# Linear attention with a rational FFN on one core: k'v of two head pairs in one visit to TensorE

## The chip, the cores and the metric

The kernel runs on one core of a Trainium2 chip. The metric is the device time of one execution in microseconds (us). Before the change the median of three runs is 900.26 us (900.21 to 900.27). The engines are named as in the profile: PE is TensorE (PEld its weight loads), ACT is ScalarE, DVE is VectorE, POOL is GpSimd, and SP is the engine whose queue issues nearly all transfers here.

## The reference

Eight batches of eight heads, 576 positions, head size 64. Attention without a softmax, an RMS norm over the head, and a feed-forward layer whose activation is a rational function:

```python
kv = np.einsum('bhsd,bhse->bhde', k, v)
out = np.einsum('bhsd,bhde->bhse', q, kv)
rms = np.sqrt(np.mean(out * out, axis=-1, keepdims=True) + 1e-06)
attn = out / rms * g_norm
x = attn.transpose(0, 2, 1, 3).reshape(4608, 512)
h = x @ w_in                                   # 512 -> 2048
P = a[0] + a[1] * h + a[2] * h**2 + a[3] * h**3
Q = 1.0 + np.abs(b[0]) * np.abs(h) + np.abs(b[1]) * h**2
return (P / (Q + 1e-06)) @ w_out               # 2048 -> 512
```

All inputs and the output are float32.

## The kernel before

**Tiles and slots.** The 4608 tokens are nine tiles of 512 (`NTILE`, numbered `t` = 0 to 8). The 2048 columns of the hidden layer are 16 chunks of 128 (`NF`), and one chunk of one tile is a *slot*; there are 144 of them, run in order. In a slot PE makes `gemm1` of the next slot (the 128x512 tile `h`, four pieces of the contraction) and `gemm2` of the slot two back (`LAG = 2`; four sub-tiles `acc`). ACT and DVE meanwhile turn `h` into the rational function `g` (`ew_a` to `ew_d`). From tile 1 on every operand of the two products is split into a high part in fp32r and a remainder (`xh`, `xl`; `gh`, `gl`; and so for the weights), and a product is three matmuls: 12 for `gemm1` and 12 for `gemm2` in a slot. Tile 0 uses plain float32 matmuls; a plain float32 matmul shows as two records in the profile.

**Attention.** While tile `t` goes through its 16 slots, the attention of tile `t + 1` is made in between, by the table `attention` (`attention0` in tile 0), which puts steps into slots. The eight heads are four pairs `p` (`NPAIR`), and the tile is made of parts of two batches, `t - 1` and `t` (64·t tokens of the older one). The steps:

- `att_kv`, in slots 0, 2, 4, 6 for pairs 0 to 3 (1, 3, 5, 7 in tile 0): the product k'v of batch `t`, pair `p`. For each of five pieces `c` of 128 positions and each head `j` of the pair, one plain float32 matmul of 128 rows by 64 columns, so ten matmuls (20 records), into columns 0 to 63 of the PSUM tile `kvp`; head `j` goes to partitions 64·j to 64·j + 63. Then ACT makes the high part `qh` of the query tile and two casts `kvh` (`split_kv`), and DVE the remainders `kvl` and `ql`. Only batches 1 to 7 are left by then (`NB` = 8; batch 0 is done in a prologue), so tile 8 has queries and no k'v.
- `att_o`, one slot later: the product q·k'v of that pair (`op`), its square and its copy `xf`. It shares one PSUM buffer (tag `at`) with `kvp`.
- `att_ms`, `att_rstd`, `att_rd`, `att_rb`, `att_norm` in slots 8 to 13: the norm, whose factor goes through DRAM to be broadcast. In slot 14, `split` makes the high and low part of the finished `x`.

Work that a step leaves to DVE is a closure that `ew_c` calls between its own three instructions (`rest[0]` to `rest[2]`; `fillat` gives the place). Nothing reorders the instructions: each engine runs them in the order written.

**Loads.** One 640 KB transfer brings k and v of a pair into `kvm` (one buffer, `bufs=1`), one of 256 KB the queries into `qr` (one buffer). `fetch_next` issues both for the next pair on SP's queue: right after the pair's `qh` is made, or in tile 0, where no split of q is made, after its `att_o`. SP waits at an issue until the buffer is free, and later issues wait behind it.

Names in a row, such as `kvp_0_1936`, end in the pair (or sub-tile, or chunk) and a serial number; the tile number isn't shown.

Of the kernel before, what the change touches and what calls it, by code (L numbers as in the profile page):

```python
# [7 lines left out]
F32 = mybir.dt.float32  # L8
F32R = mybir.dt.float32r
# [5 lines left out]
ALU = mybir.AluOpType  # L15
# [9 lines left out]
def linear_attention_then_rational_ffn(  # L25
# [9 lines left out]
    nc = tc.nc  # L35
    PE, ACT, DVE, POOL = nc.tensor, nc.scalar, nc.vector, nc.gpsimd

    NB, NPAIR = kv.shape[:2]
    NT, DM = out.shape
    NF = w_in.shape[0]  # L40
    P = 128
    D = 64
    S = NT // NB
    TW = 512
    NTILE = NT // TW
# [7 lines left out]
    work = ctx.enter_context(tc.tile_pool(name="work", bufs=2))  # L53
# [3 lines left out]
    ps_at = ctx.enter_context(tc.tile_pool(name="ps_at", bufs=2, space=PSUM))  # L57
# [14 lines left out]
    kvf = wpool.tile([P, 2, NPAIR, P], F32, tag=f"f{NF - 1}", name="kvf")  # L72
# [40 lines left out]
    kvh = [const.tile([P, P], F32R, name=f"kvh{i}") for i in range(NKV)]  # L113
    kvl = [const.tile([P, P], F32R, name=f"kvl{i}") for i in range(NKV)]
# [4 lines left out]
    def f32(t):  # L119
        return t.bitcast(F32)  # L120
# [26 lines left out]
    def at_slot(step, k):  # L147
        return [u for u in units if schedule[u][step] == k]
# [19 lines left out]
    def fetch_w(u):  # L168
        kind, c = u
        k = units.index(u) % NG  # L170
        raws[u] = wpool.tile([P, 2 * DM], I64, tag=f"g{k}", name=f"raw_{kind}{c}")
        src = w_in[c:c + 2].rearrange("c p k f -> p c (k f)") if kind == "wi" else \
            w_out[c:c + 2].rearrange("c p f -> p c f")
        to = raws[u].rearrange("p (c f) -> p c f", c=2)
        for js in ((slice(0, 1), slice(1, 2)) if u in units[:2] else (slice(0, 2),)):
            nc.sync.dma_start(to[:, js], src[:, js])
# [84 lines left out]
    def split_kv(t, p, ps):  # L261
        n = kvslot[t, p] = (t * NPAIR + p) % NKV
        for j in range(2):
            js = slice(j * D, (j + 1) * D)
            ACT.copy(kvh[n][js, js], ps[js, 0:D])
            if t == 1:
                ACT.copy(kvf[js, 1, p, js], ps[js, 0:D])

        if t == 1:

            for j in range(2):
                js = slice(j * D, (j + 1) * D)
                POOL.tensor_tensor(kvl[n][js, js], kvf[js, 1, p, js], f32(kvh[n][js, js]), ALU.subtract)
            return None

        def rest():
            for j in range(2):
                js = slice(j * D, (j + 1) * D)
                DVE.tensor_tensor(kvl[n][js, js], ps[js, 0:D], f32(kvh[n][js, js]), ALU.subtract)
        return rest  # L280

    def newton_rstd(ms, r, r2):
# [20 lines left out]
        return rest  # L303

    xs, x = {}, {}
    kvq, qs, sqs, rs, rbs, xf = {}, {}, {}, {}, {}, {}

    def fetch_kvq(t, p):
        if t < NB:
            m = work.tile([P, 2, 5, P], F32, tag="kvm", name=f"kvm_{t}_{p}", bufs=1)  # L310
            nc.sync.dma_start(m, kv[t, p])
        else:
            m = None
        q = work.tile([P, TW], F32, tag="qr", name=f"qr_{t}_{p}", bufs=1)
        nc.sync.dma_start(q, qT[p, :, t * TW:(t + 1) * TW])
        kvq[t, p] = m, q

    def fetch_next(t, p):
        if p + 1 < NPAIR:
            fetch_kvq(t, p + 1)  # L320
        elif t + 1 < NTILE:
            fetch_kvq(t + 1, 0)

    def att_kv(t, p):
        m, q = kvq.pop((t, p))
        if t < NB:
            ps = ps_at.tile([P, TW], F32, tag="at", name=f"kvp_{t}_{p}", bufs=1)
            for c in range(5):
                for j in range(2):
                    js = slice(j * D, (j + 1) * D)  # L330
                    PE.matmul(ps[js, 0:D], m[:, 0, c, js], m[:, 1, c, js], start=(c == 0), stop=(c == 4))  # L331
        if t == 1:
            qs[t, p] = q
        else:
            qh = work.tile([P, TW], F32R, tag="qh", name=f"qh_{t}_{p}", bufs=1)
            ql = work.tile([P, TW], F32R, tag="ql", name=f"ql_{t}_{p}", bufs=1)
            ACT.copy(qh, q)
            qs[t, p] = qh, ql
            fetch_next(t, p)
        split_v = split_kv(t, p, ps) if t < NB else None  # L340

        def rest():
            if split_v:
                split_v()
            if t > 1:
                DVE.tensor_tensor(ql, q, f32(qh), ALU.subtract)
        return rest

    def att_o(t, p):
        ps = ps_at.tile([P, TW], F32, tag="at", name=f"op_{t}_{p}", bufs=1)  # L350
        q = qs.pop((t, p))
        n0 = D * t
        for bt, cs in ((t - 1, slice(0, n0)), (t, slice(n0, TW))):
            if cs.start == cs.stop:
                continue
            if t == 1:
                PE.matmul(ps[:, cs], kvf[:, bt, p], q[:, cs], start=True, stop=True)  # L357
                continue
            qh, ql = q
            n = kvslot[bt, p]  # L360
            PE.matmul(ps[:, cs], kvh[n], ql[:, cs], start=True, stop=False)  # L361
            PE.matmul(ps[:, cs], kvl[n], qh[:, cs], start=False, stop=False)  # L362
            PE.matmul(ps[:, cs], kvh[n], qh[:, cs], start=False, stop=True)  # L363
        sq = work.tile([P, TW], F32, tag="at", name=f"sq_{t}_{p}", bufs=4)
        xf[t, p] = xpool.tile([P, TW], F32, tag=f"xf{p}", name=f"xf_{t}_{p}")
        ACT.activation(sq, ps, AF.Square)
        ACT.copy(xf[t, p], ps)
        sqs[t, p] = sq
        if t == 1:
            fetch_next(t, p)  # L370

    def att_ms(t, _):
        rs[t] = ps_at.tile([P, TW], F32, tag="ms", name=f"ms_{t}", bufs=1)
# [39 lines left out]

    attention = {s: [] for s in range(NF)}
    for p in range(NPAIR):
        attention[2 * p].append((att_kv, p))
        attention[2 * p + 1].append((att_o, p))
        attention[(11, 12, 13, 13)[p]].append((att_norm, p))
    attention[8].append((att_ms, 0))
    attention[9].append((att_rstd, 0))  # L420
    fillat = {att_norm: 1, att_kv: 1, att_o: 1, att_rstd: 2}
    attention[10] += [(att_rd, 0), (att_rb, 0), (att_rb, 1)]

    fillat0 = {att_kv: 1}
    attention0 = {s: [] for s in range(NF)}
    for f, at in ((att_kv, [1, 3, 5, 7]), (att_o, [2, 4, 6, 8]), (att_ms, [9]), (att_rstd, [9]), (att_rd, [10]), (att_rb, [11, 11]), (att_norm, [12, 12, 13, 13])):
        for p, k in enumerate(at):
            attention0[k].append((f, p))

# [166 lines left out]
    first_x(NPAIR - 2)  # L596
    for u in at_slot(0, -1)[:1]:
        fetch_w(u)
    fetch_kvq(1, 0)
    for u in at_slot(0, -1)[1:]:  # L600
        fetch_w(u)
    ms0 = ps_at.tile([P, TW], F32, tag="ms", name="ms_0", bufs=1)
# [22 lines left out]
    for p in range(NPAIR):  # L625
        pool, tag, bufs = ((ps_h, "h", 2), (ps_h, "h", 2), (ps_at, "at", 1), (ps_at, "ms", 1))[p]
        rb = pool.tile([P, TW], F32, tag=tag, name=f"rb_0_{p}", bufs=bufs)
        ps = slice(p * Q4, (p + 1) * Q4)
# [11 lines left out]
    for i, (t, c) in enumerate(slots[:-1]):  # L640
# [6 lines left out]
        rest = {0: [], 1: [], 2: []}  # L647
# [83 lines left out]
```

## Time and profile before

| | |
|---|---|
| median of three runs | 900.26 us (900.21 to 900.27) |
| the profiled execution: its own time, its span | 900.13 us, 898.4 us |
| PE busy | 890.4 us, 99% of the span |
| DVE, ACT, POOL busy | 772.9 us (86%), 692.5 us (77%), 113.9 us (13%) |
| granted clock of PE | 0.999 |
| moved by DMA | 74.30 MB, 83 GB/s on average |

The profile is that of one execution. The span is the time from its first to its last record; 1.73 us of the execution's own time lie outside it. Rows of the timeline give the start and the duration of an instruction in us, the engine, the line of the kernel, the operation, the tile written and those read, and how many like it stand in the row. Matmuls are pipelined, so what a matmul costs is the distance from its start to the next one's, not its duration. In such rows `kvp<-kvm` are the k'v products, `h<-x,parts` and `acc<-woh,gl` the two big products, `op<-ql,kvh` q·k'v.

### The profile page before, as it was taken

How to read it: one execution, taken by the hardware profiler on the slowest of the kernel's cores; microseconds unless marked ns; L12 is line 12 of the kernel's file. 1: busy time of each engine (PE TensorE's matmuls, PEld its weight loads, DVE VectorE, ACT ScalarE, POOL GpSimd, SP SyncE). 2: the span in 40 equal slices, each digit the busy share in tenths (PEclk: the TensorE clock that was granted, in tenths of full speed). 3: DMA queues.
4: the chain of work that ended last, by engine and by line, in shares of the span. 5: the costliest groups of instructions: out<-in, count | busy, mean ns of one | idle time of the engine just before them, and what ended most of it. 6: DMA issues, size and time to landing. Idle time of an engine off the chain costs nothing.

```text
span 898.4 us, 11765 instructions
## 1 busy us (share of the span) xinstructions
PE 890.4 (99%) x4294; PEld 680.1 (76%) x4294; DVE 772.9 (86%) x1223; ACT 692.5 (77%) x1171; POOL 113.9 (13%) x95
## 2 busy tenths in 40 slices
PE   8999999999999999999999999999999999999998
PEld 5444446878887888878887888788878887888886
DVE  3987898889978898889878997799788988898887
ACT  5898878887876788677867787768767887777665
POOL 2644465653000000000000000000000000000000
PEclk9999999999999999999999999999999999999999
DMA  9964046764131203220320122111302020201001
GB/s 367 351 254 147 25 94 165 170 132 99 41 130 41 49 25 105 83 49 1 130 75 19 37 94 78 42 49 42 129 13 49 0 71 13 49 1 47 1 1 47
DMA packets 26266, 74.30 MB, mean 83 GB/s; under 512 B 2592, under 2 KB 2592, under 8 KB 26208
## 3 DMA queue, kind: packets, MB, share of 16 engines
q1 hardware_dynamic: 23328, 64.10, 21.3%
q0 software_dynamic: 2304, 8.39, 5.1%
q10 hardware_dynamic: 576, 1.05, 0.3%
q8 instruction: 34, 0.56, 0.2%
q14 instruction: 24, 0.20, 0.1%
HBM read 55.58 MB, written 9.57 MB: 73 GB/s over the span
## 4 chain that ended last, share of the span: by engine, by line
PE 95%; DVE 2%; DMA 1%; ACT 1%; issue 0%; SPq 0%; ACTq 0%; DVEq 0%
PE h L448 14%; PE h L450 13%; PE h L449 13%; PE acc L511 13%; PE acc L513 13%; PE acc L512 13%; PE acc L507 6%; PE h L444 5%; PE kvp L331 2%; DMA first<-in_first_dram 1%; PE ms L375 1%; PE op L362 1%; PE op L363 1%; PE op L361 1%; PE op L357 0%
## 5 line engine op out<-in xcount | busy, mean ns | idle before, releaser
L458 ACT ACTIVATE d<-h 128x512 f32<-128x512 f32 x143 | 85.6, 599 | 157.0 <-PE h L450 155.2
L448 PE MATMUL h<-x,parts 128*128 128x512 f32 (+1 forms) x516 | 205.0, 397 | 0.0
L450 PE MATMUL h<-x,parts 128*128 128x512 f32 (+1 forms) x516 | 200.5, 389 | 0.0
L512 PE MATMUL acc<-wol,gh 128*128 128x512 f32 x508 | 197.7, 389 | 0.0
L460 DVE SCALAR_TENSOR_TENSOR q<-d,b1abs,q 128x512 f32<-128x512 f32 x143 | 107.1, 749 | 95.5 <-ACT q L459 95.4
L449 PE MATMUL h<-x,wil 128*128 128x512 f32 (+1 forms) x388 | 150.5, 388 | 0.0
L511 PE MATMUL acc<-parts,gl 128*128 128x512 f32 x384 | 149.4, 389 | 0.0
L513 PE MATMUL acc<-parts,gh 128*128 128x512 f32 x384 | 149.4, 389 | 0.0
L448 PEld LDWEIGHTS h<-x,parts 128*128 128x128 f32 x516 | 96.9, 188 | 25.9 <-DVE gl L495 5.9
L471 ACT ACTIVATE d<-q,bias 128x512 f32<-128x512 f32 x143 | 105.3, 737 | 12.7 <-DVE q L460 10.9
L450 PEld LDWEIGHTS h<-x,parts 128*128 128x128 f32 x516 | 96.9, 188 | 20.6
L461 ACT ACTIVATE u<-h,na 128x512 f32<-128x512 f32 x143 | 112.0, 783 | 0.0
L512 PEld LDWEIGHTS acc<-wol,gh 128*128 128x128 f32 x508 | 95.4, 188 | 19.8
L472 ACT ACTIVATE d<-d,bias 128x512 f32<-128x512 f32 x143 | 103.6, 725 | 4.7
L468 DVE SCALAR_TENSOR_TENSOR u<-u,na,h 128x512 f32<-128x512 f32 x143 | 106.1, 742 | 0.6
L478 DVE SCALAR_TENSOR_TENSOR u<-u,na,d 128x512 f32<-128x512 f32 x143 | 106.5, 744 | 0.0
L462 DVE TENSOR_TENSOR u<-u,h 128x512 f32<-128x512 f32 x143 | 97.8, 684 | 0.8
L476 DVE SCALAR_TENSOR_TENSOR q<-q,d 128x512 f32<-128x512 f32 x143 | 98.3, 687 | 0.2 <-ACT d L472 0.2
L459 ACT ACTIVATE q<-h,abg 128x512 f32<-128x512 f32 x143 | 97.9, 685 | 0.0
L484 DVE SCALAR_TENSOR_TENSOR u<-q,u 128x512 f32<-128x512 f32 x127 | 91.7, 722 | 2.4
L495 DVE TENSOR_TENSOR gl<-u,gh 128x512 fp32r<-128x512 f32 x127 | 86.8, 683 | 0.0
L449 PEld LDWEIGHTS h<-x,wil 128*128 128x128 f32 x388 | 73.0, 188 | 13.8
(146 smaller groups left out, 1234.6 us busy)
## 6 DMA issues: line engine op xcount, KB each, us to landing
kvm<-in_kv_dram SPq DMA_DIRECT2D x28, 640.0 KB
raw_wo<-in_w_out_dram SPq DMA_DIRECT2D x8, 1024.0 KB
qr<-in_qT_dram SPq DMA_DIRECT2D x32, 256.0 KB
out_dram<-ob SPq DMA_DIRECT2D x16, 512.0 KB
rb<-rd SPq DMA_DIRECT2D x28, 256.0 KB
raw_wi<-in_w_in_dram SPq DMA_DIRECT2D x6, 1024.0 KB
wol<-wow POOLq DMA_DIRECT2D x8, 512.0 KB, 5.2
wil<-wiw POOLq DMA_DIRECT2D x6, 512.0 KB, 4.6
```

The source lines that it names most:

```text
L448: PE.matmul(ph, wh, xl, start=(kc == 0), stop=False)
L449: PE.matmul(ph, wl, xh, start=False, stop=False)
L450: PE.matmul(ph, wh, xh, start=False, stop=(kc == NPAIR - 1))
L460: q_made = DVE.scalar_tensor_tensor(q, d, b1abs, q, ALU.mult, ALU.add)
L461: ACT.activation(u, ph, AF.Identity, bias=na[:, 2:3], scale=na[:, 3:4])
L468: DVE.scalar_tensor_tensor(u, u, na[:, 1:2], ph, ALU.add, ALU.mult)
L471: ACT.activation(d, q, AF.Ln, bias=bias[:, 2:3], scale=QSC)
L472: ACT.activation(d, d, AF.Exp, bias=bias[:, 3:4], scale=-1.0)
L478: DVE.scalar_tensor_tensor(u, u, na[:, 0:1], d, ALU.add, ALU.mult)
L511: PE.matmul(o, gl[:, ss], wh, start=(c == 0), stop=False)
L512: PE.matmul(o, gh[:, ss], wl, start=False, stop=False)
L513: PE.matmul(o, gh[:, ss], wh, start=False, stop=(c == NF - 1))
```

## The change

The two k'v products of pairs 0 and 1 are made in one visit in slot 0 of a tile, and those of pairs 2 and 3 in slot 4 (`att_kv2`), each into its own 64 columns of one PSUM tile. The queries keep their slots 0, 2, 4 and 6 (`att_q`). k and v get two buffers, by the parity of the pair (`kvm0`, `kvm1`), and are fetched two pairs at a time; the queries are fetched for themselves. In tile 0, where the attention of tile 1 is made, k'v stays one pair to a visit (`att_kv1`).

```diff
 def split_kv(t, p, ps):        # ps is now the 64 columns of the pair
-            ACT.copy(kvh[n][js, js], ps[js, 0:D])
+            ACT.copy(kvh[n][js, js], ps[js])
...
+    def fetch_kv(t, p):
+        kvms[t, p] = work.tile([P, 2, 5, P], F32, tag=f"kvm{p % 2}", name=f"kvm_{t}_{p}", bufs=1)
+        nc.sync.dma_start(kvms[t, p], kv[t, p])
+
+    def fetch_q(t, p):
+        qrs[t, p] = work.tile([P, TW], F32, tag="qr", name=f"qr_{t}_{p}", bufs=1)
+        nc.sync.dma_start(qrs[t, p], qT[p, :, t * TW:(t + 1) * TW])
+
+    def fetch_first_kv(t):
         if t < NB:
+            for p in range(2):
+                fetch_kv(t, p)
...
+    def kv_products(t, ps, k, p):
+        m = kvms.pop((t, p))
+        for c in range(5):
+            for j in range(2):
+                js = slice(j * D, (j + 1) * D)
+                PE.matmul(ps[js, k * D:(k + 1) * D], m[:, 0, c, js], m[:, 1, c, js], start=(c == 0), stop=(c == 4))
...
+    def att_kv2(t, g):
+        if t >= NB:
+            return None
+        ps = ps_at.tile([P, TW], F32, tag="at", name=f"kvp_{t}_{g}", bufs=1)
+        for k in range(2):
+            kv_products(t, ps, k, 2 * g + k)
+        if g == 0:
+            for p in (2, 3):
+                fetch_kv(t, p)
         else:
+            fetch_first_kv(t + 1)
+        splits = [split_kv(t, 2 * g + k, ps[:, k * D:(k + 1) * D]) for k in range(2)]
         def rest():
+            for f in splits:
+                f()
+        return rest
+
+    def att_q(t, p):
+        q = qrs.pop((t, p))
+        qh = work.tile([P, TW], F32R, tag="qh", name=f"qh_{t}_{p}", bufs=1)
+        ql = work.tile([P, TW], F32R, tag="ql", name=f"ql_{t}_{p}", bufs=1)
+        ACT.copy(qh, q)
+        qs[t, p] = qh, ql
+        fetch_next_q(t, p)
...
 in att_o:
         if t == 1:
-            fetch_next(t, p)
+            if p + 1 < NPAIR:
+                fetch_kv(t, p + 1)
+            else:
+                fetch_first_kv(t + 1)
+            fetch_next_q(t, p)
...
     for p in range(NPAIR):
-        attention[2 * p].append((att_kv, p))
+        if p % 2 == 0:
+            attention[2 * p].append((att_kv2, p // 2))
+        attention[2 * p].append((att_q, p))
         attention[2 * p + 1].append((att_o, p))
```

PE's order around slot 0 of the tile in which batch 3 is prepared, before and then after (`kvp` is the PSUM tile of k'v, `kvm` the loaded k and v, `acc` and `h` the results of `gemm2` and `gemm1`):

```order
L511 MATMUL acc_3_1141<-woh_1648,gl_14_1875 128x512
L512 MATMUL acc_3_1141<-wol_1677,gh_14_1874 128x512
L513 MATMUL acc_3_1141<-woh_1648,gh_14_1874 128x512
L331 MATMUL kvp_0_1936<-kvm_0_1427 64x64 x10
L448 MATMUL h_1_1956<-x_0_1853,parts_847 128x512
L449 MATMUL h_1_1956<-x_0_1853,parts_859 128x512
```

```order
L538 MATMUL acc_3_1159<-woh_1648,gl_14_1875 128x512
L539 MATMUL acc_3_1159<-wol_1677,gh_14_1874 128x512
L540 MATMUL acc_3_1159<-woh_1648,gh_14_1874 128x512
L332 MATMUL kvp_0_1936<-kvm_0_1306 64x64 x10
L332 MATMUL kvp_0_1936<-kvm_1_1308 64x64 x10
L475 MATMUL h_1_1970<-x_0_1853,parts_849 128x512
L476 MATMUL h_1_1970<-x_0_1853,parts_861 128x512
```

The ten matmuls of pair 1, from the second buffer, now follow those of pair 0 directly. On the same engine, two slots later, before and after:

```order
L512 MATMUL acc_3_2055<-wol_929,gh_0_1983 128x512
L513 MATMUL acc_3_2055<-parts_913,gh_0_1983 128x512
L331 MATMUL kvp_1_2068<-kvm_1_1950 64x64 x10
L448 MATMUL h_3_2088<-x_0_1853,parts_847 128x512
L449 MATMUL h_3_2088<-x_0_1853,parts_859 128x512
```

```order
L539 MATMUL acc_3_2071<-wol_931,gh_0_1999 128x512
L540 MATMUL acc_3_2071<-parts_915,gh_0_1999 128x512
L475 MATMUL h_3_2089<-x_0_1853,parts_849 128x512
L476 MATMUL h_3_2089<-x_0_1853,parts_861 128x512
L477 MATMUL h_3_2089<-x_0_1853,parts_849 128x512
```

Here `gemm1` now follows `gemm2` with nothing in between. On DVE, at the end of that slot 0 (`kvl` and `ql` are the remainders of k'v and q, `u` the rational function's numerator), before and after:

```order
L478 SCALAR_TENSOR_TENSOR u_0_1911<-u_0_1911,na,d_0_1909 128x512
L279 TENSOR_TENSOR kvl_131<-kvp_0_1936,kvh_125 64x64 x2
L346 TENSOR_TENSOR ql_0_1948<-qr_0_1429,qh_0_1947 128x512
L484 SCALAR_TENSOR_TENSOR u_0_1911<-q_0_1910,u_0_1911 128x512
L460 SCALAR_TENSOR_TENSOR q_1_1976<-d_1_1975,b1abs,q_1_1976 128x512
```

```order
L505 SCALAR_TENSOR_TENSOR u_0_1911<-u_0_1911,na,d_0_1909 128x512
L279 TENSOR_TENSOR kvl_131<-kvp_0_1936,kvh_125 64x64 x2
L279 TENSOR_TENSOR kvl_132<-kvp_0_1936,kvh_126 64x64 x2
L367 TENSOR_TENSOR ql_0_1966<-qr_0_1433,qh_0_1965 128x512
L511 SCALAR_TENSOR_TENSOR u_0_1911<-q_0_1910,u_0_1911 128x512
L487 SCALAR_TENSOR_TENSOR q_1_1992<-d_1_1991,b1abs,q_1_1992 128x512
```

The two subtractions of the second pair have come ahead of `ql`; two slots later they are gone. On ACT the four casts `kvh` now stand ahead of the cast `qh`, where the two stood behind it.

More of the change, by code (lines that the diff above doesn't have):

```diff
@@ L264, in split_kv @@
             js = slice(j * D, (j + 1) * D)
-            ACT.copy(kvh[n][js, js], ps[js, 0:D])
+            ACT.copy(kvh[n][js, js], ps[js])
             if t == 1:
-                ACT.copy(kvf[js, 1, p, js], ps[js, 0:D])
+                ACT.copy(kvf[js, 1, p, js], ps[js])
         if t == 1:
@@ L278, in rest @@
                 js = slice(j * D, (j + 1) * D)
-                DVE.tensor_tensor(kvl[n][js, js], ps[js, 0:D], f32(kvh[n][js, js]), ALU.subtract)
+                DVE.tensor_tensor(kvl[n][js, js], ps[js], f32(kvh[n][js, js]), ALU.subtract)
         return rest
@@ L305, in linear_attention_then_rational_ffn @@
     xs, x = {}, {}
-    kvq, qs, sqs, rs, rbs, xf = {}, {}, {}, {}, {}, {}
-    def fetch_kvq(t, p):
-        if t < NB:
-            m = work.tile([P, 2, 5, P], F32, tag="kvm", name=f"kvm_{t}_{p}", bufs=1)
-            nc.sync.dma_start(m, kv[t, p])
-        else:
[L313 to L338, printed above, removed]
-            fetch_next(t, p)
-        split_v = split_kv(t, p, ps) if t < NB else None
-        def rest():
[L343 to L346, printed above, removed]
+    kvms, qrs, qs, sqs, rs, rbs, xf = {}, {}, {}, {}, {}, {}, {}
@@ new lines, in fetch_kv, with fetch_next_q @@
+    def fetch_kv(t, p):
[5 more added lines that the diff above has]
+    def fetch_first_kv(t):
+        if t < NB:
+            for p in range(2):
+                fetch_kv(t, p)
+    def fetch_next_q(t, p):
+        if p + 1 < NPAIR:
+            fetch_q(t, p + 1)
+        elif t + 1 < NTILE:
+            fetch_q(t + 1, 0)
@@ new lines, in kv_products, with att_kv1 @@
+    def kv_products(t, ps, k, p):
[4 more added lines that the diff above has]
+                PE.matmul(ps[js, k * D:(k + 1) * D], m[:, 0, c, js], m[:, 1, c, js], start=(c == 0), stop=(c == 4))
+    def att_kv1(t, p):
+        ps = ps_at.tile([P, TW], F32, tag="at", name=f"kvp_{t}_{p}", bufs=1)
+        kv_products(t, ps, 0, p)
+        qs[t, p] = qrs.pop((t, p))
+        split_kv(t, p, ps[:, 0:D])
+    def att_kv2(t, g):
[7 more added lines that the diff above has]
+                fetch_kv(t, p)
+        else:
+            fetch_first_kv(t + 1)
+        splits = [split_kv(t, 2 * g + k, ps[:, k * D:(k + 1) * D]) for k in range(2)]
+        def rest():
+            for f in splits:
+                f()
+        return rest
@@ L347, in att_kv, with rest @@
+    def att_q(t, p):
[5 more added lines that the diff above has]
+        fetch_next_q(t, p)
+        def rest():
+            DVE.tensor_tensor(ql, q, f32(qh), ALU.subtract)
         return rest
@@ L369, in att_o @@
         if t == 1:
-            fetch_next(t, p)
+            if p + 1 < NPAIR:
+                fetch_kv(t, p + 1)
+            else:
+                fetch_first_kv(t + 1)
+            fetch_next_q(t, p)
     def att_ms(t, _):
@@ L420, in linear_attention_then_rational_ffn @@
     attention[9].append((att_rstd, 0))
-    fillat = {att_norm: 1, att_kv: 1, att_o: 1, att_rstd: 2}
+    fillat = {att_norm: 1, att_kv2: 1, att_q: 1, att_rstd: 2}
     attention[10] += [(att_rd, 0), (att_rb, 0), (att_rb, 1)]
-    fillat0 = {att_kv: 1}
+    fillat0 = {}
     attention0 = {s: [] for s in range(NF)}
-    for f, at in ((att_kv, [1, 3, 5, 7]), (att_o, [2, 4, 6, 8]), (att_ms, [9]), (att_rstd, [9]), (att_rd, [10]), (att_rb, [11, 11]), (att_norm, [12, 12, 13, 13])):
+    for f, at in ((att_kv1, [1, 3, 5, 7]), (att_o, [2, 4, 6, 8]), (att_ms, [9]), (att_rstd, [9]), (att_rd, [10]), (att_rb, [11, 11]), (att_norm, [12, 12, 13, 13])):
         for p, k in enumerate(at):
@@ L598, in linear_attention_then_rational_ffn @@
         fetch_w(u)
-    fetch_kvq(1, 0)
+    fetch_kv(1, 0)
+    fetch_q(1, 0)
     for u in at_slot(0, -1)[1:]:
```

## The prediction

> **What bounds the kernel now.** I read the page first, then the table by stages, then the waits of the stretch that the change works in. The page, its engines and the chain that ended last:
>
> ```profile
> span 898.4 us, 11765 instructions
> PE 890.4 (99%) x4294; PEld 680.1 (76%) x4294; DVE 772.9 (86%) x1223; ACT 692.5 (77%) x1171; POOL 113.9 (13%) x95
> PE 95%; DVE 2%; DMA 1%; ACT 1%; issue 0%; SPq 0%; ACTq 0%; DVEq 0%
> ```
>
> PE is busy for 99% of the span and carries 95% of the chain. An average hides stages, so the same by stretch (duration; then busy us and count of PE, PEld, DVE, ACT, POOL; clock, DMA share, GB/s): tile 0, one middle tile, and the last in which k'v is made.
>
> ```profile
> 0.00:139.00 139.00, 135.22 (x517) 66.44 (x518) 110.73 (x169) 111.86 (x171) 67.15 (x72) 1.00 0.58 204
> 234.00:330.00 96.00, 96.00 (x501) 78.00 (x500) 83.96 (x136) 73.23 (x129) 0.00 (x0) 1.00 0.20 61
> 617.00:712.00 95.00, 95.00 (x493) 77.23 (x492) 82.14 (x134) 71.67 (x126) 0.00 (x0) 1.00 0.18 55
> ```
>
> In a middle tile PE has no idle time in 96 us, at full clock. Who waits there (from 235 to 810 us: total us, times, longest)?
>
> ```profile
> ACT d L458 <- PE h L450: 124.5, 79, 2.9
> DVE q L460 <- ACT q L459: 68.1, 65, 2.0
> PEld h L448 <- DVE gl L495: 5.0, 6, 0.8
> ```
>
> ACT waits for PE's `h`, and DVE for ACT. The third row is weight loads, not matmuls, that start later, 0.8 us a tile at most. So PE's own sequence sets the time: a us taken out of PE's stream is a us off the end, as long as DVE and ACT keep their reserve.
>
> **What a visit costs PE.** The first visit of that middle tile, with what stands around it, and two slots' joint with no visit, for the normal distance:
>
> ```profile
> 237.40 0.39 PE L512 MATMUL acc<-wol,gh 128*128 128x512 f32 x1
> 237.62 0.39 PE L513 MATMUL acc<-woh,gh 128*128 128x512 f32 x1
> 237.94 0.80 PE L331 MATMUL kvp<-kvm 128*64 128x64 f32 x20
> 238.67 0.50 PE L448 MATMUL h<-x,parts 128*128 128x512 f32 x1
> 239.01 0.39 PE L449 MATMUL h<-x,parts 128*128 128x512 f32 x1
> ...
> 316.38 0.39 PE L512 MATMUL acc<-wol,gh 128*128 128x512 f32 x1
> 316.61 0.39 PE L513 MATMUL acc<-parts,gh 128*128 128x512 f32 x1
> 316.84 0.39 PE L448 MATMUL h<-x,parts 128*128 128x512 f32 x1
> 317.06 0.39 PE L449 MATMUL h<-x,wil 128*128 128x512 f32 x1
> ```
>
> The normal distance from one matmul to the next is 0.227 us (316.38 to 317.06 is three of them), and where `gemm1` follows `gemm2` directly it is the same. Around a visit it isn't: 0.32 from L513 to the first k'v record (0.09 too much), 0.73 from there to L448, and 0.34 from L448 to L449 (0.11 too much). From L513 to L449 it is 1.39 us where 0.455 would be two normal steps: **a visit costs 0.93 us**, of which 0.20 are entry and exit. The last visit has the same distances:
>
> ```profile
> 657.72 0.39 PE L513 MATMUL acc<-parts,gh 128*128 128x512 f32 x1
> 658.04 0.80 PE L331 MATMUL kvp<-kvm 128*64 128x64 f32 x20
> 658.77 0.50 PE L448 MATMUL h<-x,parts 128*128 128x512 f32 x1
> 659.11 0.39 PE L449 MATMUL h<-x,wil 128*128 128x512 f32 x1
> ```
>
> Of the 0.73 a part is fixed too. The 20 records start in ten couples (head 0 and head 1 together). A window shorter than the visit shows only the records in flight in it: the first row is the window 237.90 to 238.03, the second 238.50 to 238.70.
>
> ```profile
> 237.94 0.28 PE L331 MATMUL kvp<-kvm 128*64 128x64 f32 x2
> 238.28 0.46 PE L331 MATMUL kvp<-kvm 128*64 128x64 f32 x10
> ```
>
> The second row is the last five couples: from 238.28 until 238.74, less the 0.222 of one record, they start within 0.24 us, four steps of 0.059. The first five take 238.28 - 237.94 = 0.34 us, which is four such steps and 0.11 for the first: 0.05 too much. From the start of the last couple (238.52) to L448 it is 0.15, or 0.09 too much. So of 0.73 about 0.585 are ten steps of 0.0585, and 0.145 are the start and the end of a run.
>
> **The change part by part.**
>
> *Visits on PE.* Batches 2 to 7 have four visits each, 24, and will have 12 of double length (batch 1, made in tile 0, stays at four single ones). If the second ten matmuls follow the first at the step of 0.0585, a double visit costs 0.93 + 0.585 = 1.515 us where two single ones cost 1.86: 0.35 us less. 12 x 0.35 = **4.2 us off PE**. The trace has no run of 40 such records, so the bounds: at best exactly this, since 20 more records at the steady step can't be had for less; if the second ten pay the start and end of a run again (0.145), only entry and exit are saved, 12 x 0.20 = 2.4 us. The worse end is among the rivals. I take 4.2: in the visit itself the weight loads change at every record without a loss after the first, and the change of heads, pieces and accumulation starts costs none; the second ten differ by buffer, columns and one wait for a transfer long landed.
>
> *Slots 2 and 6* lose their visit whole; the joint is that of 316.61, at 0.227. That is in the sum already.
>
> *DVE and ACT in slots 0 and 4.* No instruction is added, two casts and two subtractions move two slots ahead. The rows of slot 0, then the op that needs the results and the next user of `gl`:
>
> ```profile
> 239.68 0.60 ACT L337 CAST qh<-qr 128x512 fp32r<-128x512 f32 x1
> 240.19 0.42 ACT L265 CAST kvh<-kvp 64x64 fp32r<-64x64 f32 x2
> 241.73 0.60 ACT L458 ACTIVATE d<-h 128x512 f32<-128x512 f32 x1 [1.13 <-PE h L450]
> ```
>
> ```profile
> 241.30 0.45 DVE L279 TENSOR_TENSOR kvl<-kvp,kvh 64x64 fp32r<-64x64 f32 x2
> 241.76 0.69 DVE L346 TENSOR_TENSOR ql<-qr,qh 128x512 fp32r<-128x512 f32 x1
> 242.37 0.68 DVE L484 SCALAR_TENSOR_TENSOR u<-q,u 128x512 f32<-128x512 f32 x1
> 242.97 0.74 DVE L460 SCALAR_TENSOR_TENSOR q<-d,b1abs,q 128x512 f32<-128x512 f32 x1
> 244.35 0.68 DVE L495 TENSOR_TENSOR gl<-u,gh 128x512 fp32r<-128x512 f32 x1
> ```
>
> ```profile
> 244.25 0.25 PE L361 MATMUL op<-ql,kvh 128*128 128x192 f32 x1
> 247.77 0.39 PE L511 MATMUL acc<-parts,gl 128*128 128x512 f32 x1
> ```
>
> ACT has 0.42 us more and waits 1.13 us for `h` afterwards; that `h` comes 0.585 later still. The four casts now need PE's visit ended: about 239.5 (237.94 + 0.73 + 0.585, and 0.2 for the last record), before ACT reaches them at 239.68. DVE has 0.46 us more before `ql`: it ends at 242.9 instead of 242.45. `op` needs it at 244.25 + 0.585, so of a reserve of 1.8 us nothing is lost. `gl` ends at 245.5 instead of 245.03 and is needed at 247.77 or later: 2.7 us of reserve. The same work leaves slots 2 and 6, where PE's slot gets 0.93 shorter and DVE's 0.46. Cost on PE: nothing; with the cover gone it would be up to 0.46 us a visit, 5.5 us.
>
> *Loads.* 28 transfers of k and v stay 28, and those of q 32. SP now issues two loads behind a visit and q behind them:
>
> ```profile
> 238.78 0.37 SPq L311 DMA_DIRECT2D kvm<-in_kv_dram  x1
> 242.53 0.36 SPq L315 DMA_DIRECT2D qr<-in_qT_dram  x1
> ...
> 251.43 0.35 SPq L311 DMA_DIRECT2D kvm<-in_kv_dram  x1
> ```
>
> ```profile
> q1 hardware_dynamic: 23328, 64.10, 21.3%
> 251.90 0.60 ACT L337 CAST qh<-qr 128x512 fp32r<-128x512 f32 x1
> ```
>
> SP's queue moved 64.10 MB in 21.3% of 898.4 us, 335 KB in a us, so by that rate the 1.31 MB of two loads take 3.9 us and q 0.8. q isn't issued before its buffer is free (242.53 now), lands some 1 to 5 us later, and is used at 251.90. The pairs 2 and 3 are used in slot 4, over 20 us after their issue, and the pairs of the next batch some 12 slots after theirs. In tile 0 the loads of k and v come up sooner, for want of a wait for the one buffer, by less than a visit and a slot; the big weight loads stay behind the same waits of q. I cost all of this at nothing: a late load would show as idle PE, and no row of a middle tile is near it.
>
> **The sum:** 900.13 - 4.2 = 895.9 us for the profiled execution, whose time is 0.13 below the median of 900.26; against that, **896.1 us**. It stands or falls with 12 x 0.35.
>
> **The rivals.**
>
> *A second start (898).* The second ten matmuls begin like a visit of their own, without entry and exit. For it: the first couple's lost 0.05 is that of weights not loaded ahead, and the wait for the second buffer's transfer stands on the weight load. Against it: `gemm1`'s first matmul carries a wait in every slot (316.61 to 316.84) at no loss. 900.3 - 2.4 = 897.9 us.
>
> *PE isn't fed fast enough (slower).* In the present visit 20 records and 20 weight loads go by in under 0.6 us after PE worked through matmuls of 0.227 us, in which the next instructions could pile up. 40 in a row may outrun that pile. Had every couple of the second ten the first one's 0.11 instead of 0.0585, a visit would get 0.49 us longer and the 0.35 would be gone: 12 x 0.14 = 1.7 us, 902.0 us. It decides from a step of 0.093 on. For it: no row with a longer run of these. Against it: within 20 the step doesn't grow towards the end (0.059 in the last five).
> The Trainium skill speaks for this rival: its page "TensorE: Matmul & The Clock Gate" gives TensorE a queue of 64 entries (the table at its head) and, where the hardware doesn't decode, some 62 ns to issue one matmul (Part 1). Taken so, the first 32 of the 40 records would come from the queue and the last eight at 62 ns, an estimate from that page of 0.26 us a visit and 3.1 us in all, so a time of 899.2; no run here shows it so far.
>
> *DVE or ACT becomes late (899 to 901).* DVE goes from slot 0 into slot 1 without a pause (242.37 to 242.97), and slot 0 gets 0.46 us more. If half of that came through to PE at slot 0 alone, 6 x 0.23 = 1.4 us would go. Against it stand the reserves of 1.8 and 2.7 us.
>
> **How the numbers follow.** Full saving 0.66 (895.6 to 896.6); a second start 0.18 (897 to 898.4); not fed 0.08 (898.5 to 902.5); DVE or ACT late 0.05; something else 0.03. The first two hold 0.84, so the range is 895.6 to 898.4. A difference of 0.2%, 1.8 us, is about what a measurement can tell from none; full saving (0.47%) and second start (0.27%) lie beyond it. Faster 0.85, within it 0.11, slower 0.04.
>
> **What would show it.** Right: rows of 40 k'v records, 1.31 us from the first to the `gemm1` matmul behind it, 0.32 before and 0.34 after; 0.227 from `gemm2` to `gemm1` in slots 2 and 6; a middle tile 0.70 us shorter; PE still without idle time. A distance of 1.46 means a second start, 1.6 or more a PE that isn't fed. The prediction is wrong if matmuls `op` or `acc` come to wait for `ql`, `kvl` or `gl`, or a visit for `kvm`.

## The result, and the profile after

The changed kernel takes **895.63 us** (median of four runs, 895.59 to 895.84) against 900.26 us: 4.6 us less. Timed once more in a series of its own it took 895.51 us against 900.17 us, ratio 0.9949 (95% interval 0.9937 to 0.9961). The prediction was 896.1 us, with 895.6 to 898.4 as range. The times below are medians of each series without the one execution, in four of them, that took far longer (3103.06 us in the loads alone, 2345.40 in the run of 80, 2309.58 with less leaving, 1274.84 in the five-fold subtractions, this last at a mean granted clock of 0.655).

The page of the changed kernel, in the parts shown of before:

```profile
span 893.8 us, 11734 instructions
PE 886.1 (99%) x4294; PEld 680.1 (76%) x4294; DVE 774.0 (87%) x1223; ACT 696.6 (78%) x1171; POOL 114.4 (13%) x95
PE 97%; DMA 1%; DVE 1%; ACT 0%; issue 0%; SPq 0%; DVEq 0%; ACTq 0%
```

PE has the same 4294 matmuls and 4.3 us less of busy time; DVE and ACT have the same number of instructions as before. The chain is still PE's. The timeline of PE around the double visit of slot 0 in the tile looked at before, and then the same joint in slot 2, where a visit used to stand:

```profile
236.88 0.39 PE L540 MATMUL acc<-woh,gh 128*128 128x512 f32 x1
237.20 1.39 PE L332 MATMUL kvp<-kvm 128*64 128x64 f32 x40
238.51 0.50 PE L475 MATMUL h<-x,parts 128*128 128x512 f32 x1
238.85 0.39 PE L476 MATMUL h<-x,parts 128*128 128x512 f32 x1
...
250.10 0.39 PE L540 MATMUL acc<-parts,gh 128*128 128x512 f32 x1
250.32 0.39 PE L475 MATMUL h<-x,parts 128*128 128x512 f32 x1
250.55 0.39 PE L476 MATMUL h<-x,parts 128*128 128x512 f32 x1
```

40 records in a row, 0.32 us in, 1.31 us through, 0.34 us out, each as foretold. From L540 to L476 it is 1.97 us, less two normal steps 1.515: the double visit costs what the sum had. In slot 2 `gemm1` follows `gemm2` at 0.22 to 0.23. The seam between the two pairs lies near 237.8. A window from 237.79 to 237.86 shows the records in flight around it:

```profile
237.59 0.46 PE L332 MATMUL kvp<-kvm 128*64 128x64 f32 x10
```

Ten records, from 237.59 to 238.05; less the 0.22 of the last, five couples start within 0.24 us, four steps of 0.059, as in the middle of a single visit. The second ten matmuls begin without a loss. The wait for the second buffer's load on their first weight load costs nothing that can be seen.

DVE and ACT in slot 0, and the matmul that needs their results:

```profile
238.89 0.85 ACT L265 CAST kvh<-kvp 64x64 fp32r<-64x64 f32 x4
240.51 0.92 DVE L279 TENSOR_TENSOR kvl<-kvp,kvh 64x64 fp32r<-64x64 f32 x4
241.47 0.69 DVE L367 TENSOR_TENSOR ql<-qr,qh 128x512 fp32r<-128x512 f32 x1
244.09 0.25 PE L382 MATMUL op<-ql,kvh 128*128 128x192 f32 x1
```

`ql` ends at 242.16, 1.93 us ahead of `op`; 1.8 was foretold. Who waits from 235 to 805 us:

```profile
ACT d L485 <- PE h L477: 115.7, 79, 2.9
ACT kvh L265 <- PE kvp L332: 1.6, 5, 0.3
```

The wait of `gemm1`'s weight loads for DVE's `gl` is 5.0 us in all, as before. The second row is new: in slot 4 of five tiles ACT comes to the casts 0.3 us before PE's visit has ended. ACT still waits for PE's `h` afterwards, and nothing follows from it.

### The profile page after: what moved, and what is told of

Read it like the earlier page. It is cut to its first block, busy times and chain, and to the rows that moved or that the text cites. A ratio compares the mean times of both kernels' runs of the same rounds, so it can differ in the third digit from the quotient of the medians.

```text
span 893.8 us, 11734 instructions
## 1 busy us (share of the span) xinstructions
PE 886.1 (99%) x4294; PEld 680.1 (76%) x4294; DVE 774.0 (87%) x1223; ACT 696.6 (78%) x1171; POOL 114.4 (13%) x95
## 4 chain that ended last, share of the span: by engine, by line
PE 97%; DMA 1%; DVE 1%; ACT 0%; issue 0%; SPq 0%; DVEq 0%; ACTq 0%
PE h L475 14%; PE h L477 13%; PE h L476 13%; PE acc L538 13%; PE acc L539 13%; PE acc L540 13%; PE acc L534 6%; PE h L471 5%; PE kvp L332 2%; DMA first<-in_first_dram 1%; PE ms L400 1%; PE op L383 1%; PE op L384 1%; PE op L382 1%; PE op L378 0%; DVE x L658 0%
## 5 line engine op out<-in xcount | busy, mean ns | idle before, releaser
L477 PE MATMUL h<-x,parts 128*128 128x512 f32 (+1 forms) x516 | 200.3, 388 | 0.0
L476 PE MATMUL h<-x,wil 128*128 128x512 f32 (+1 forms) x388 | 150.4, 388 | 0.0
L540 PE MATMUL acc<-parts,gh 128*128 128x512 f32 x384 | 149.4, 389 | 0.0
L477 PEld LDWEIGHTS h<-x,parts 128*128 128x128 f32 x516 | 96.9, 188 | 20.5
L521 ACT CAST gh<-u 128x512 fp32r<-128x512 f32 x127 | 80.3, 632 | 4.1 <-DVE u L511 4.1
```

Of the source, the lines that this page charges most:

```text
L476: PE.matmul(ph, wl, xh, start=False, stop=False)
L477: PE.matmul(ph, wh, xh, start=False, stop=(kc == NPAIR - 1))
L540: PE.matmul(o, gh[:, ss], wh, start=False, stop=(c == NF - 1))
```

## The experiments

Each is made from the changed kernel unless it says otherwise, and was timed beside the kernel before.

**The change again.**

> The changed kernel once more, to be compared with the three beside it. Theory (each visit of TensorE to the k'v products has a fixed price of 0.35 us beside 0.0585 us for a couple of records): 895.6 us, 4.2 to 4.7 us below the kernel before. Rival (part of the gain is a matter of the single execution): a gain that differs by over 0.5 us from the 4.6 us seen.

895.51 us, 4.66 below the 900.17 of its series: the gain is that of the kernel, not of one execution.

**The loads alone.** k'v of one pair to a visit again, with the new buffers and fetches:

```diff
+    def att_kv2(t, p):
...
+        kv_products(t, ps, 0, p)
+        if p == 1:
+            for o in (2, 3):
+                fetch_kv(t, o)
+        elif p == 3:
+            fetch_first_kv(t + 1)
...
-        if p % 2 == 0:
-            attention[2 * p].append((att_kv2, p // 2))
+        attention[2 * p].append((att_kv2, p))
```

> The loads of the change (k and v in two buffers and fetched two pairs at a time, q for itself) with k'v still made one pair to a visit, in slots 0, 2, 4 and 6. Theory (the visits are all of it): 900.3 us, the kernel before within 0.2 us. Rival (the earlier loads or the new order of SP's queue carry the 0.45 us that the gain is above the 4.2 us foretold): 899.8 us. Each visit should again take 0.32 us in, 0.73 us, and 0.34 us out.

900.1 us, ratio 0.9999 (0.9990 to 1.0008): the kernel before. Buffers and order of SP's queue are worth nothing by themselves, and the rival that gave them the rest of the gain is out.

**The two pairs apart.** Half of `gemm2` is put between them:

```diff
-            gemm2(*slots[i - LAG])
+            first_of_two = t >= 1 and t + 1 < NB and c in (0, 4)
+            gemm2(*slots[i - LAG], between=(lambda: early_kv(t + 1, c // 4)) if first_of_two else None)
```

> All of the change, but the two pairs of a visit stand apart on TensorE: pair 0 (or 2) in the middle of the slot's gemm2, pair 1 (or 3) behind it; loads, ACT and DVE as in the change. Theory (a fixed price for each stay): 12 stays more at 0.35 to 0.38 us, 899.8 to 900.2 us, with slots 2 and 6 still free of k'v. Rival (the gain comes of slots 2 and 6 being free, or of DVE's and ACT's work standing elsewhere): 895.6 us.

900.15 us, ratio 0.9999 (0.9991 to 1.0008). The whole gain is gone, though slots 2 and 6 are free, ACT and DVE work as in the change, and the same loads are made. PE's timeline of slot 0:

```profile
236.19 0.39 PE L547 MATMUL acc<-woh,gh 128*128 128x512 f32 x1
236.51 0.80 PE L332 MATMUL kvp<-kvm 128*64 128x64 f32 x20
237.24 0.50 PE L545 MATMUL acc<-woh,gl 128*128 128x512 f32 x1
237.58 0.40 PE L546 MATMUL acc<-wol,gh 128*128 128x512 f32 x1
```

0.32, 0.73 and 0.34 again, now with `gemm2` on both sides. The price is for a stay, wherever it stands.

**A run of 80.** The products of a visit are made twice over:

```diff
-        for k in range(2):
-            kv_products(t, ps, k, 2 * g + k)
+        for again in range(2):
+            for k in range(2):
+                kv_products(t, ps, k, 2 * g + k, keep=again == 0)
```

> Each visit makes its products twice over into the same columns, 80 records in a row instead of 40; the second pass overwrites the first with the same values. Theory (the step of 0.0585 us a couple holds for any length): 12 x 20 couples x 0.0583 = 14.0 us more than the change, 909.6 us, one step throughout. Rival (TensorE isn't fed fast enough in a long run, which 40 records just did not show): the steps grow towards the end of the run; at 0.124 us a couple for the last 24 couples it would be 12 x 24 x 0.066 = 19 us more still, 928 us.

909.48 us, 14.0 us above the change.

```profile
239.52 2.55 PE L332 MATMUL kvp<-kvm 128*64 128x64 f32 x80
242.00 0.50 PE L476 MATMUL h<-x,parts 128*128 128x512 f32 x1
```

80 records take 2.48 us where 40 took 1.31: 20 couples more in 1.17 us, 0.0585 each. The step doesn't grow, so PE is fed fast enough for a run of twice the length of the change's. The estimate that the prediction drew from the Trainium skill's page "TensorE: Matmul & The Clock Gate", records beyond a queue of 64 entries at 62 ns each, isn't borne out by this run.

**The array undivided.** k'v as five matmuls a pair of 128 by 128, of which the diagonal blocks are used:

```diff
-            kv_products(t, ps, k, 2 * g + k)
+            m = kvms.pop((t, 2 * g + k))
+            for c in range(5):
+                PE.matmul(ps[:, k * P:(k + 1) * P], m[:, 0, c], m[:, 1, c], start=(c == 0), stop=(c == 4))
```

> k'v as products of the whole pair, 128 rows by 128 columns, of which the two blocks on the diagonal are used: five matmuls a pair that use the array undivided, ten records where there were twenty. Records of 128 columns in plain float32 come at 0.111 us in the prologue, so a visit's run is 20 x 0.111 = 2.2 us instead of 1.17 us plus its start and end. Theory (entry, exit, start and end are paid for the change of the array's division): none of them, a visit of 2.2 us instead of 1.516 us, 12 x 0.7 = 8.4 us more than the change, 904.0 us, and the matmul ahead of gemm1 at a normal distance. Rival (they are paid for going from fp32r to plain float32 and back, or for any change of operands): 12 x 0.35 = 4.2 us on top, 908.2 us.

904.13 us, where 904.0 was expected and the rival had 908.2.

```profile
238.30 0.39 PE L543 MATMUL acc<-woh,gh 128*128 128x512 f32 x1
238.53 2.39 PE L348 MATMUL kvp<-kvm 128*128 128x128 f32 x20
240.67 0.48 PE L478 MATMUL h<-x,parts 128*128 128x512 f32 x1
240.99 0.40 PE L479 MATMUL h<-x,parts 128*128 128x512 f32 x1
```

The entry is a normal 0.23 us. From L543 to L479 it is 2.69 us, less two normal steps 2.24, which is 20 records at 0.112: no fixed price is left. Plain float32 between fp32r matmuls costs nothing by itself; what costs is going to the 64-column division of the array and back. The records of this form are longer too, but that isn't it: the matmuls `ms` (shown further down), longer still and in a division of 32 columns, have the same 0.32 and 0.34 around them. The Trainium skill, on its page "TensorEngine Tiling (Array Packing)", under Key Properties, states that a change of tiling mode drains the engine; these runs agree and put 0.35 us on a stay in another division. The undivided form has no such price and is still dearer here, since a pair takes 1.12 us in it instead of 0.585.

The weight loads show where the price arises. The first two rows are the way in and out of the first visit in the trace before, the third the way in of the undivided form:

```profile
237.94 0.66 PEld L331 LDWEIGHTS kvp<-kvm 128*64 128x64 f32 x20 [0.35 <-PE acc L511]
238.67 0.19 PEld L448 LDWEIGHTS h<-x,parts 128*128 128x128 f32 x1
```

```profile
238.30 2.42 PEld L348 LDWEIGHTS kvp<-kvm 128*128 128x128 f32 x20
```

In the stream, and in the undivided form too, a weight load starts a whole matmul (0.22 us) ahead of its own: at 238.30 for the matmul of 238.53 (on the way out of the undivided form it is 0.03 us ahead). Where the division changes it starts only with its matmul, at 237.94 and at 238.67, and so it is at every visit and every `ms` of a middle tile in the traces of before, of the change, of the pairs apart and of the two versions with fewer breaks.

**DVE's reserve.** The four subtractions `kvl` two, five and then four times over:

```diff
-            for f in splits:
-                f()
+            for _ in range(2):
+                for f in splits:
+                    f()
```

> DVE makes the four subtractions kvl of a visit twice (the same result again), 0.92 us more ahead of ql in slots 0 and 4. Theory (DVE has 1.9 us in slot 0 and 2.8 us in slot 4 before TensorE's q.k'v needs ql): no change, 895.6 us. Rival (DVE's work in these slots reaches TensorE, so that the change lost part of its gain there): up to 12 x 0.92 = 11 us more, 906.7 us.

895.61 us: 0.9 to 1.1 us more on DVE in twelve slots is hidden whole.

> DVE makes the four subtractions kvl of a visit five times, 3.7 us more ahead of ql in slots 0 and 4: beyond the reserve as read from the trace of the change. Theory (the reserve is 1.9 us in slot 0 and 2.8 us in slot 4): TensorE waits 1.8 us in slot 1 and 0.9 us in slot 5 for ql, 6 x 2.7 = 16 us, 911 us. Rival (the reserve is larger, since the work ahead would move up): 896 us; or smaller: up to 12 x 3.7 = 44 us.

924.12 us, 13 us above what was expected. The reserve was read rightly, and other things came on top. DVE and PE of slots 0 and 1 in one tile:

```profile
245.74 5.03 DVE L279 TENSOR_TENSOR kvl<-kvp,kvh 64x64 fp32r<-64x64 f32 x20
```

```profile
251.54 0.36 PE L383 MATMUL op<-ql,kvh 128*128 128x192 f32 x1 [2.11 <-DVE ql L368]
...
252.88 0.44 PE L478 MATMUL h<-x,parts 128*128 128x512 f32 x1
253.12 0.63 PE L476 MATMUL h<-x,parts 128*128 128x512 f32 x1
253.55 0.63 PE L477 MATMUL h<-x,parts 128*128 128x512 f32 x1
```

The subtractions take 5.03 us instead of 0.92, 4.11 more (3.7 expected), and PE waits 2.11: a reserve of 2.0 us (1.9 expected). But 1.6 us after the wait the matmuls come 0.43 us apart instead of 0.227. The table by stretch (columns as before, the clock is the third number from the end):

```profile
253.10:256.50 3.40, 3.40 (x9) 2.67 (x8) 3.37 (x6) 3.37 (x7) 0.00 (x0) 0.50 0.24 89
257.00:262.00 5.00, 5.00 (x23) 4.12 (x22) 3.72 (x6) 4.28 (x8) 0.00 (x0) 1.00 0.40 149
550.92:555.00 4.08, 4.08 (x20) 3.51 (x21) 4.05 (x7) 3.42 (x7) 0.00 (x0) 1.00 0.21 64
```

For 3.4 us PE's granted clock is 0.50, with PE busy throughout: some 1.7 us more lost for a wait of 2.1. This comes in three of the six tiles that have double visits, from 253.1, 352.1 and 451.1 us; in the other three, waits of 2.16, 1.98 and 1.99 us (until 179.22, 550.92 and 649.65) have no drop behind them. The last row is the stretch behind the wait until 550.92. Of the 13 us some 5 are the clock, some 5 the longer subtractions in twelve slots, and the rest tile 1 and the restarts behind the waits. The four-fold version asks how short a wait does this.

> The four subtractions kvl four times, 3.1 us more ahead of ql. The reserve that the five-fold version showed is 2.0 us in slot 0 and 2.7 us in slot 4. Theory (TensorE's clock falls only behind a wait as long as that version's 2.1 us): waits of 1.1 and 0.4 us in six tiles, 9 us more than the change, 904.5 us, the clock at 1.0 throughout. Rival (each wait draws a stretch of half speed behind it): another 1.9 us for each longer wait, 916 us.

907.18 us, between the two. The clock stays at 1.00 in every stretch: behind the longest wait of a middle tile,

```profile
248.59 0.36 PE L383 MATMUL op<-ql,kvh 128*128 128x192 f32 x1 [1.10 <-DVE ql L368]
```

the matmuls go on at 0.227. So the theory holds on the clock, and its sum was too small elsewhere. In a middle tile the start of `gemm1` falls back by 1.23 to 1.35 us in slot 1 (the wait of 1.1, and a restart) and 0.41 to 0.43 us in slot 5, near the 1.5 expected; in tile 1, where ACT and DVE still split the weights, by 3.3 us. The reserve is smaller there, which the expectation left out.

**Less leaving.** The visit for pairs 0 and 1 goes to slot 8 of the tile before, right ahead of `ms`, which uses 32 columns:

```diff
-        if p % 2 == 0:
-            attention[2 * p].append((att_kv2, p // 2))
+        if p == 2:
+            attention[2 * p].append((att_kv2, 1))
...
-    attention[8].append((att_ms, 0))
+    attention[8] += [(lambda t, g: att_kv2(t + 1, g), 0), (att_ms, 0)]
...
+            for step, p in ([(att_kv2, 0)] if (t, c) == (1, 0) else []) + (attention0 if t == 0 else attention)[c]:
```

> The visit for pairs 0 and 1 moves from slot 0 to slot 8 of the tile before, right ahead of the matmuls ms, which use the array in another division (32 columns where k'v uses 64); batch 2 keeps its visit in slot 0. Six of twelve visits then have ms behind them instead of gemm1. Theory (what is paid is the break in the stream of 128-column matmuls, once when it is left and once when it is taken up again): six leavings and takings-up fewer, each pair worth 0.35 to 0.38 us, less a change from 64 to 32 columns of some 0.15 us: 894.1 to 894.7 us. Rival (every change of division has the full price): 895.6 us.

894.41 us, ratio to the kernel before 0.9936 (0.9923 to 0.9949), 1.1 us less than the change.

```profile
286.43 0.39 PE L541 MATMUL acc<-parts,gh 128*128 128x512 f32 x1
286.75 1.39 PE L332 MATMUL kvp<-kvm 128*64 128x64 f32 x40
288.06 1.06 PE L401 MATMUL ms<-sq,sel 128*32 128x512 f32 x8
289.06 0.50 PE L476 MATMUL h<-x,parts 128*128 128x512 f32 x1
289.39 0.40 PE L477 MATMUL h<-x,wil 128*128 128x512 f32 x1
```

The rows have one entry of 0.32 and one exit of 0.33 for both. The way from L541 to L477 is 2.96 us. In the changed kernel `ms` stands alone, and from L540 to L476 it is 1.65:

```profile
286.68 0.39 PE L540 MATMUL acc<-parts,gh 128*128 128x512 f32 x1
287.00 1.06 PE L400 MATMUL ms<-sq,sel 128*32 128x512 f32 x8
287.99 0.50 PE L475 MATMUL h<-x,parts 128*128 128x512 f32 x1
288.33 0.39 PE L476 MATMUL h<-x,wil 128*128 128x512 f32 x1
```

The visit beside it thus costs 1.31 us here instead of 1.515: 0.2 us saved at each. They are five, one for each of the batches 3 to 7, and not the six that the expectation counted.

**k'v ahead of q·k'v.** On top of that, the visit for pairs 2 and 3 moves ahead of `op` in slot 3:

```diff
-        if p == 2:
-            attention[2 * p].append((att_kv2, 1))
+        if p == 1:
+            attention[3].append((att_kv2, 1))
...
-        ps = ps_at.tile([P, TW], F32, tag="at", name=f"kvp_{t}_{g}", bufs=1)
+        ps = ps_at.tile([P, TW], F32, tag=("at", "ms")[g], name=f"kvp_{t}_{g}", bufs=1)
```

> On top of the version with the visit beside ms (894.41 us): the visit for pairs 2 and 3 moves from slot 4 to slot 3, right ahead of the q.k'v matmuls of pair 1, into the PSUM buffer of ms, with a seventh buffer for kvh and kvl. Theory (each break in the stream of 512-column matmuls is paid once, 0.11 us at its end and 0.03 us over the next five matmuls, whatever stands in it): six breaks fewer, 0.03 to 0.14 us each, 893.6 to 894.2 us. Rival (the price belongs to the kind of matmul, so the q.k'v matmuls pay it in gemm1's place): 894.4 us or more.

894.14 us, ratio to the kernel before 0.9933 (0.9920 to 0.9947): the fastest of all, at the weak end of its expectation.

```profile
255.50 1.39 PE L332 MATMUL kvp<-kvm 128*64 128x64 f32 x40
256.81 0.36 PE L383 MATMUL op<-ql,kvh 128*128 128x192 f32 x1
257.00 0.28 PE L384 MATMUL op<-qh,kvl 128*128 128x192 f32 x1
...
257.68 0.39 PE L476 MATMUL h<-x,parts 128*128 128x512 f32 x1
257.91 0.39 PE L477 MATMUL h<-x,wil 128*128 128x512 f32 x1
```

The first matmul of `op` takes 0.19 us where it takes 0.08 behind `gemm2`. So `op` pays the 0.11 in `gemm1`'s place, as the rival had it; only about the 0.03 of the theory is saved (0.25 us over the six visits in the traces), since `gemm1` follows `op` at 0.23.

## Why the prediction was right

*That PE's own sequence sets the time:* shown. Buffers and loads alone gave nothing, twice the subtractions cost nothing, and 14.0 us more of matmuls gave 14.0 us more.

*A visit has a fixed price of 0.35 us, in entry, exit, start and end of a run:* shown. It comes back whole when the pairs stand apart, and goes whole when the array isn't divided. The choice between the bounds, steady step against a second start, is settled by the seam and by the run of 80.

*12 x 0.35 = 4.2 us:* the term that was mis-sized, by a tenth. The prediction had called 4.2 the best that could be had, and 895.63 lies only just inside its range. The gain is 4.6 us, and a middle tile got shorter by 0.77 us, not 0.70: from the first visit of one tile to that of the next it was 95.31 us before (237.94 to 333.25) and is 94.54 now (237.20 to 331.74).

```profile
333.25 0.34 PE L331 MATMUL kvp<-kvm 128*64 128x64 f32 x4
```

```profile
331.74 0.34 PE L332 MATMUL kvp<-kvm 128*64 128x64 f32 x4
```

The prediction stopped at the second matmul behind a visit, and the price doesn't. This is the seventh `gemm1` matmul behind the visit of slot 0 in the trace before, and its like in slot 2 of the trace after, where no visit stands ahead:

```profile
240.17 0.39 PE L448 MATMUL h<-x,parts 128*128 128x512 f32 x1
```

```profile
251.69 0.39 PE L475 MATMUL h<-x,parts 128*128 128x512 f32 x1
```

Before, from the second (239.01) to the seventh it is 1.16 us; after, from 250.55, it is 1.14, and in the records' nanoseconds the five steps differ by 26 in all. With that a stay costs 0.38 us and not 0.35, and 12 x 0.38 = 4.6 us. By the starts of `gemm1` in every slot, before against after, a double visit adds 0.584 us to its slot, and a slot freed of its visit gains 0.824 at its start and 0.136 behind; with 0.004 less at the exit of a double visit that is 0.38 for each of the twelve, or 4.56. The changed kernel is 0.03 us ahead before its first double visit, and 0.05 are lost behind a short wait at the end of tile 1 that the trace before has too. Together that is the 4.54 us between the two profiled executions (900.13 and 895.59).

That short wait shows what the exit and the tail are. In the trace before, the weights of one `gemm2` matmul wait 0.26 us for DVE's `gl` there, with no k'v and no other division near:

```profile
235.00 0.19 PEld L511 LDWEIGHTS acc<-woh,gl 128*128 128x128 f32 x1 [0.26 <-DVE gl L495]
```

```profile
235.00 0.50 PE L511 MATMUL acc<-woh,gl 128*128 128x512 f32 x1
235.33 0.39 PE L512 MATMUL acc<-wol,gh 128*128 128x512 f32 x1
```

The weight load starts with its matmul, the next matmul follows at 0.335 us, and the five steps behind it are 231, 236, 228, 233 and 230 ns; behind the visit of slot 0 it is 0.339 us, and then 231, 236, 228, 233 and 231 ns. So the 0.11 and the tail go with a matmul whose weights weren't loaded ahead, whatever held them up, and a change of division is one such thing. This is read from the rows; no run varied it by itself. Why the single steps come 1 to 9 ns late is open.

*DVE, ACT and the loads at nothing:* right, with the reserve of 1.8 us measured as 1.9 to 2.0. No wait of PE for `kvm`, `ql`, `kvl` or `gl` was added.

*The rivals:* a second start is refuted by the seam, a PE that isn't fed by the run of 80, DVE or ACT being late by the doubled subtractions.

## What to carry to other kernels

On an engine that never waits, look at the distances between starts around a short guest in its stream, not at the guest's duration: here 0.35 of 0.93 us were the price of coming and going. Put guests that use another division of the array together, and next to others that leave the undivided array too, before making them shorter. Measure the distances for some matmuls beyond the guest, since the price has a tail, and look at where the weight loads start: one that starts with its matmul instead of ahead of it marks the price.

## What the runs showed that was not expected

In the five-fold version a wait of some 2 us on PE cost nearly twice its length in three of six tiles: the granted clock fell to 0.50 for 3.413 us and came back by itself. In the other three tiles, behind waits as long, it stayed at 1.00, and so it did behind the waits of 1.1 us in the four-fold version. The length of a wait alone thus doesn't decide. The drops start at 253.09, 352.08 and 451.07 us, 98.99 us apart, which is 29 times 3.413. If time is divided into stretches of 3.413 us in step with them, the stretch ahead of each drop held 1.86, 1.98 and 1.98 us of waiting, while each of the other three waits falls into two stretches, with at most 1.37 us in one. That fits a clock that follows the idle time in fixed stretches; it is a reading of one trace, and no run tested it. The Trainium skill, on its page "TensorE: Matmul & The Clock Gate" (Part 1), has the clock halved after an idle window of some 3.4 us; here a window that was idle for little more than half was enough, and the measurement decides.

The price of taking the stream up again isn't tied to `gemm1`: the first 128-column matmul behind a visit, behind `ms`, behind the wait at 235.00, and (in the version with `op` behind the visit) the first of `op` all take about 0.11 us more.
